# Weight sums and inverse softmax sums moved into the gate phase of a fused attention and GeGLU block

## The chip, the cores and the metric

The kernel runs on one core of one Trainium2 chip. The metric is the device time of one execution in microseconds (us), as the median of several runs. A separate, profiled execution gives the trace that is read here. Its engines are TensorE (PE; its weight loads are shown apart as PEld), VectorE (DVE), ScalarE (ACT), GpSimd (POOL) and SyncE (SP), whose queue issues all the transfers (DMA) that matter here.

## The reference

A block of 2048 tokens of width 640 is normalised, and two branches read the result: sliding-window attention of 32 heads of 20 (window 256), and a gated feed-forward part (GeGLU) of width 1728. Both are added to the input.

```python
qkv = (xn @ wqkv).reshape(B, S, 3, H, Dh)...
p = softmax(where(mask, q @ k.T * Dh ** -0.5, -1e9))
attn = (p @ v).reshape(B, S, D) @ wo
h = gelu(xn @ w_gate) * (xn @ w_up)
return x + attn + h @ w_down
```

All is float32. The kernel gets that precision from reduced-precision matmuls by splitting each operand into a high half (rounded) and a low half (the remainder), and adding three products: high by high, low by high, high by low.

## The kernel before

**Stages.** First the layer norm and the projections, with attention; parts of the gate and up projections are filled in between the attention's matmuls. Attention leaves, for each chunk c of 512 tokens, its unnormalised output in DRAM (`od[c]`, 640 rows) and the softmax sums (`sd[c]`, 32 heads). Then comes the *gate phase*, which computes the remaining feed-forward tiles f = 6 to 12 of 128 features and writes each to DRAM (`hd[f][c]`). Last, the *output phase* multiplies [h, attention output] with the stacked weights [w_down; wo] and adds x.

**Gate phase.** `gate_up_pair(f, w, p, extra)` handles tile f for the chunks 2p and 2p + 1, as a Winograd form of a 2 by 2 block product (fewer products, more sums): 54 matmuls of 128x128 by 512 (L858), into the banks pa, pb, pc, pe. Each tile has a first pair (p = 0) and a second (p = 1). VectorE adds up the results (`add`, L861): g1 from pb, `qp` from pc, then from pe, g2 from pc, u from pe. PE adds to the bank of pc a second time, so it must wait for the first `qp` sum. The products h2 and h1 (L891, L893) are stored by SP (L892, L894). `extra[i]` are functions put at four *hooks*, `more(0)` to `more(3)`, inside the pair, one for each quarter: there the next tile's weights are split (GpSimd makes their low halves) and summed, and in the last pair (f = 12, p = 1) the first work of the output phase is done.

**Output phase.** The stacked weights form nine *quads* q = 0 to 8. A quad is two blocks of 128 rows, each cut into two halves of 320 columns: four tiles of 128x320 (640 KB). There are eight groups p of 256 tokens, and a group has nine *steps*, one for each quad, and a small step "e" for the last 64 features (weights `w13`). Steps are counted n = 0, 1, ... through all groups. The quads 0 to 5 and the first block of quad 6 belong to h, the other five blocks to the attention output (`od`), which must be multiplied with the inverse softmax sums.

- Group 0 is *plain*: in a step four tiles of the quad as they are (kind "b"), 24 matmuls (L1023) into the banks 2, 3, 4, 8.
- The other groups are Winograd: 21 matmuls a step into seven banks, with three tiles of the quad and four *sums* of its tiles (kind "t"), and on the activation side with three parts and four sums `ss`. A group has 197 matmuls of 320 columns, step e among them; the plain group has 224.

`load_step(n)` loads a step's activations from `hd` and `od` (`hr`, 256 KB, L979). `split_step(n)` multiplies what comes from `od` with `rb` (the inverse sums, spread over the rows) on GpSimd (L1001), then makes high halves on ScalarE (L1003 in the plain group, L1007 and L1012 in Winograd ones) and sums and low halves on VectorE (the helper `sub`, L944). `fetch` loads a quad, `high_quad` (L929, L931) makes its high halves on ScalarE, `low_quad` (L941) its low halves on VectorE or GpSimd, and `sums_quad` turns the loaded tiles into the four sums in place (four subtractions of 128x320, VectorE, L944), which are split again as kind "t". All this is done in the steps 0 to 9: in the steps 1 to 5 a quad is split, summed and split again, in one step; in the steps 6 to 9 the quads 0 to 3, fetched a second time, are summed and split. `drain` adds a group's banks to x and stores it (L1053 and others; one of its sums is on GpSimd).

The inverse sums are made in the gate phase by `norm_items`: load `sd[c]`, reciprocal on VectorE, store to `rd[c]`. `load_rb` reads `rd[c]` back, spread, once for each chunk of the output phase (L984).

**What sets the order.** Within each phase, the order on PE, ScalarE, VectorE and the SP queue is that in which the program is written (`manual_schedule`), save that a few of the output phase's first splits stand inside the last gate pair. Every engine and the SP queue works in order: an instruction that waits holds all behind it. Transfers share eight semaphores in turn, so one waits until the eighth before it has landed.

**The loop of the output phase**, for each n: at the group's fourth step load x, then `load_step(n + 4)`, `split_step(n + 2)`, `prepare(n)` (the quad work of this step), and the matmuls, `terms`.

Of the kernel before, what the change touches and what calls it, by code (L numbers as in the profile page):

```python
# [60 lines left out]
def block_kernel(ctx, tc, x, wqk, wv, wgu, wdo, wdl, out):  # L61
# [22 lines left out]
    td = [{i: dram.tile([128, 2, C], F32, name=f"td{p}{i}") for i in (1, 2, 3, 4)} for p in range(NC // 2)]  # L84
    rd = [dram.tile([H, C], F32, name=f"rd{c}") for c in range(NC)]
# [671 lines left out]
    def norm_items(c):  # L757
        st = {}

        def n1():  # L760
            st["rc"] = c2.tile([128, 128], F32, name="rc", tag="rc", bufs=2)
            nc.sync.dma_start(st["rc"], sd[c].rearrange("h (a t) -> (h a) t", a=4))

        def n2():
            nc.vector.reciprocal(st["rc"], st["rc"])

        def n3():
            nc.sync.dma_start(rd[c].rearrange("h (a t) -> (h a) t", a=4), st["rc"])

        return n1, n2, n3  # L770

# [127 lines left out]
    borrow = {7: 0, 3: 4}  # L899

    def new_quad(kind, q):
        tag = place.get((kind, q))
        quads[kind, q] = (xp if tag else rp3).tile([128, 2, 4, HD], F32R, name=f"w{kind}{q}", tag=tag or f"w{kind}{q}")

    def slots(kind, q):
        if kind == "t" and q in borrow:
            return [(quads["b", borrow[q] + i], slice(1, 2), slice(i, i + 1)) for i in range(4)]
        if (kind, q) not in quads:
            new_quad(kind, q)
        return [(quads[kind, q], slice(0, 4), slice(0, 4))]  # L910

    def fetch(q, pool, tag, bufs):
        if pool is None:
            staged[q] = [wrp.tile([128, KT, 128], F32, name="wr", tag="wr") for _ in range(2)]
            staged[q] = [t.rearrange("p k m -> p (k m)").rearrange("p (h n) -> p h n", h=2) for t in staged[q]]
            for i, t in enumerate(staged[q]):
                nc.sync.dma_start(t, wdo[q][:, i].rearrange("p (h n) -> p h n", h=2))
        else:
            t = pool.tile([128, 4, HD], F32, name="stg", tag=tag, bufs=bufs)
            nc.sync.dma_start(t, wdo[q].rearrange("p k (h n) -> p (k h) n", h=2))  # L920
            staged[q] = [t]

    def high_quad(kind, q):
        n = 4 // len(staged[q])
        for i, raw in enumerate(staged[q]):
            for t, dst, src in slots(kind, q):
                if len(staged[q]) > 1:
                    dst = src = slice(n * i, n * i + n)
                    nc.scalar.activation(t[:, 0, dst], raw, AF.Copy)  # L929
                else:  # L930
                    nc.scalar.activation(t[:, 0, dst], raw[:, src], AF.Copy)  # L931

    def low_quad(kind, q, eng):
        n = 4 // len(staged[q])
        for i, raw in enumerate(staged[q]):
            for t, dst, src in slots(kind, q):
                if len(staged[q]) > 1:
                    dst = slice(n * i, n * i + n)
                else:
                    raw = staged[q][0][:, src]  # L940
                eng.tensor_tensor(out=t[:, 1, dst], in0=raw, in1=t[:, 0, dst].bitcast(F32), op=OP.subtract)  # L941
# [18 lines left out]
    for p in range(NP):  # L960
        ks_ = list(range(NQD))
        if p % 2:
            ks_ = ks_[4:] + ks_[:4]
        steps += [(p, k) for k in ks_[:4] + ["e"] + ks_[4:]]
    rbs = {}
# [15 lines left out]
    def load_rb(c):  # L981
        rbs[c] = cp.tile([128, C], F32, name="rb", tag="rb")
        for i in range(4):
            nc.sync.dma_start(rbs[c][32 * i:32 * i + 32], rd[c])  # L984

    def split_step(n):
# [11 lines left out]
        for i in range(2):  # L998
            if 2 * k + i >= NF - 1:
                a = raw[:, 2 * i:2 * i + 2].rearrange("p a t -> p (a t)")  # L1000
                nc.gpsimd.tensor_tensor(out=a, in0=a, in1=rbs[c][:, t0:t0 + 256], op=OP.mult)  # L1001
        if p == 0:
# [13 lines left out]
    def terms(n, ps, begin, end):  # L1016
# [3 lines left out]
        def mul(bank, parts):  # L1020
            last = len(parts) - 1
            for j, (a, b) in enumerate(parts):
                nc.tensor.matmul(ps[bank][:, 0:HD], a, b, start=begin and j == 0 and (k != "e"),  # L1023
                                 stop=end and j == last, skip_group_check=True)

        if k == "e":
            for bank, tok, h in ((2, 1, 0), (3, 1, 1), (4, 0, 0)):
                mul(bank, [(t[:, tok], w13[:, z, h * HD:h * HD + HD]) for z in range(2)])
            for z in range(2):
                nc.tensor.matmul(ps[8][:, 0:HD], t[:, 0], w13[:, z, HD:D], start=p > 0 and z == 0,  # L1030
                                 stop=p > 0 and z == 1, skip_group_check=True)
# [8 lines left out]
        if p == 0:  # L1040
# [3 lines left out]
        for bank, a, w, b in ((1, 0, wb, 0), (2, 2, wb, 2), (4, 1, None, 2), (5, 3, None, 0), (6, 4, None, 3),  # L1044
                              (7, 5, None, 1), (3, 6, wb, 3)):
            mul(bank, three(a, w, b))

    def drain(p, ps, xt):
# [18 lines left out]
        add(1, 1, a, nc.gpsimd)  # L1067
# [11 lines left out]
        add(2, 2, a)  # L1079
        store(2, 2)  # L1080
# [47 lines left out]
    for j, f in enumerate(range(NFA, NF - 1)):  # L1128
        end = f + 1 == NF - 1
        first, second = {i: [] for i in range(4)}, {i: [] for i in range(4)}  # L1130
        if j < NC:
            start_norm(j)
# [146 lines left out]
```

## Time and profile before

| what | value |
| --- | --- |
| median of 3 runs | 1148.94 us (1147.72 to 1149.1) |
| the profiled execution, own time | 1152.38 us |
| its span, first to last instruction | 1150.7 us |
| mean granted TensorE clock | 0.973 of full |
| PE busy | 1088.6 us (95%) |
| DVE busy | 757.4 us (66%) |
| ACT busy | 512.4 us (45%) |
| POOL busy | 403.7 us (35%) |
| moved by DMA | 136.75 MB, mean 119 GB/s |

How to read the views quoted below. The page cuts the span in 40 slices of 28.8 us and gives for each the busy share of every engine in tenths, and the granted TensorE clock in tenths. A view by windows has one line for each stretch: its length, then busy us (and number of instructions) of PE, PEld, DVE, ACT, POOL, then granted clock, DMA share and GB/s. A line of the waits reads: engine and tile that waited, whom it waited for, us in total, times, longest. A line of the timeline has start and length in us, engine, line, operation, output and inputs, shape, and in brackets the idle time before it and what ended it.

### The profile page before, as it was taken

Reading aid. Unit: us, or ns where it says so; the run is one execution under the profiler, and the core shown is the slowest. Engines: PE = TensorE matmul, PEld = TensorE weight load, DVE = VectorE, ACT = ScalarE, POOL = GpSimd, SP = SyncE. Lnnn points to the kernel's source line nnn. Section 1 sums busy time; section 2 is a strip of 40 time slices with the busy share of each in tenths; the row PEclk is TensorE's granted clock in tenths of the full one; section 3 lists DMA queues with packets and bytes.
Section 4 is the critical chain, followed back from the end, with each engine's and each line's share of the span. In section 5 each row is a group of like instructions: output and inputs, shape, how many; then the busy total and the mean of one; then the engine's idle time right before and its main releaser. Section 6 shows DMA issues by size and latency. Waiting matters only on the chain.

```text
span 1150.7 us, 20894 instructions
## 1 busy us (share of the span) xinstructions
PE 1088.6 (95%) x7241; PEld 871.0 (76%) x7241; DVE 757.4 (66%) x2064; ACT 512.4 (45%) x1034; POOL 403.7 (35%) x577
## 2 busy tenths in 40 slices
PE   8999999999999999999999999999975559999998
PEld 7877666666778666666666688888864449999998
DVE  7666666666666666666666366665545478888886
ACT  4435655656545556455555552232233233333332
POOL 5036634649445336553352411111112450202020
PEclk9999999999999999999999999999986779999999
DMA  5543343455532333533322152221064233444443
GB/s 195 185 130 100 110 135 108 120 148 161 153 96 71 113 114 111 165 100 112 112 84 89 61 183 81 79 91 62 37 213 140 97 106 116 133 141 132 143 125 103
DMA packets 87226, 136.75 MB, mean 119 GB/s; under 512 B 12608, under 2 KB 57280, under 8 KB 87120
## 3 DMA queue, kind: packets, MB, share of 16 engines
q1 hardware_dynamic: 87120, 135.41, 38.0%
q8 instruction: 57, 0.93, 0.4%
q14 instruction: 49, 0.40, 0.1%
HBM read 89.98 MB, written 45.09 MB: 117 GB/s over the span
## 4 chain that ended last, share of the span: by engine, by line
PE 82%; DVE 7%; issue 4%; DMA 3%; ACT 2%; POOL 1%; SPq 1%; DVEq 0%; POOLq 0%; ACTq 0%
PE ps_d L99 22%; PE ps L1023 18%; PE ps_g L858 14%; PE ps_o L514 7%; PE ps_e L492 7%; PE ps_m L440 6%; PE ps_v L99 5%; DVE junk L442 1%; PE ps_g L99 1%; DVE at L944 1%; DMA stg<-wdo 1%; DVE stg L944 1%; ACT P L494 1%; DMA xi<-x 1%; DVE xi L158 1%
## 5 line engine op out<-in xcount | busy, mean ns | idle before, releaser
L442 DVE CUSTOM_DVE_ANT_0 junk<-ps_m,mask 128x384 bf16<-128x384 f32 (+2 forms) x512 | 271.8, 531 | 177.3 <-PE ps_m L440 136.1
L494 ACT ACTIVATE P<-ps_e 128x512 f32<-128x512 f32 (+2 forms) x384 | 197.6, 568 | 63.6 <-PE ps_e L492 57.4
L1023 PE MATMUL ps<-wb,at 128*128 128x320 f32 x951 | 162.2, 324 | 36.3 <-ACT at L1003 19.2
L1023 PEld LDWEIGHTS ps<-wb,at 128*128 128x128 f32 x951 | 151.5, 199 | 40.4 <-ACT at L1003 20.8
L500 POOL TENSOR_SCALAR_AFFINE_SELECT P<-P 128x512 f32<-128x512 f32 x128 | 84.0, 656 | 176.1 <-ACT P L494 169.2
L99 PE MATMUL ps_d<-xh,wql 128*128 128x512 f32 x430 | 129.2, 410 | 0.0
L99 PE MATMUL ps_d<-xl,wqh 128*128 128x512 f32 x430 | 128.6, 408 | 0.0
L99 PE MATMUL ps_d<-xh,wqh 128*128 128x512 f32 x430 | 128.5, 409 | 0.0
L440 PE MATMUL ps_m<-ks,qs 120*128 120x128 bf16 (+1 forms) x704 | 121.0, 275 | 3.6 <-DVE mx L442 2.0
L492 PE MATMUL ps_e<-qs,ks 122*128 122x128 bf16 (+2 forms) x704 | 113.1, 277 | 1.5 <-ACT P L494 0.8
L1023 PE MATMUL ps<-wt,at 128*128 128x320 f32 x588 | 96.1, 313 | 0.0
L492 PEld LDWEIGHTS <-ks 122*128 122x128 bf16 x704 | 50.2, 98 | 55.1 <-issue 44.4
L1023 PEld LDWEIGHTS ps<-wt,at 128*128 128x128 f32 x588 | 89.6, 191 | 0.5 <-DVE m L944 0.2
L99 PEld LDWEIGHTS ps_d<-xh,wql 128*128 128x128 f32 x430 | 77.9, 189 | 15.7 <-issue 2.3
L99 PEld LDWEIGHTS ps_d<-xl,wqh 128*128 128x128 f32 x430 | 78.3, 189 | 14.9 <-issue 0.6
L99 PEld LDWEIGHTS ps_d<-xh,wqh 128*128 128x128 f32 x430 | 77.8, 189 | 14.1 <-ACT xh L183 0.3
L440 PEld LDWEIGHTS <-qs 120*128 120x128 bf16 x704 | 62.1, 98 | 32.8 <-issue 14.0
L503 POOL TENSOR_SCALAR_AFFINE_SELECT P<-P 128x512 f32<-128x512 f32 x112 | 72.6, 658 | 37.2 <-ACT P L494 37.2
L514 PE MATMUL ps_o<-P,v 128*32 128x384 f32 (+2 forms) x1408 | 84.3, 386 | 0.0
L223 POOL TENSOR_TENSOR pt<-r,pt 128x512 bf16<-128x512 f32 x40 | 46.8, 1170 | 80.9 <-ACT pt L222 80.8
L944 DVE TENSOR_TENSOR at<-hr,at 128x384 fp32r<-128x384 f32 (+1 forms) x72 | 51.0, 708 | 34.6 <-ACT at L1003 26.0
L1012 ACT ACTIVATE at<-ss 128x512 fp32r<-128x512 f32 x63 | 39.7, 630 | 72.3 <-DVE ss L944 72.1
(180 smaller groups left out, 1765.1 us busy)
## 6 DMA issues: line engine op xcount, KB each, us to landing
hd<-he SPq DMA_DIRECT2D x52, 256.0 KB
hr<-hd SPq DMA_DIRECT2D x104, 128.0 KB
wr<-wgu SPq DMA_DIRECT2D x27, 320.0 KB
qs<-qd SPq DMA_DIRECT2D x32, 240.0 KB
ks<-kd SPq DMA_DIRECT2D x32, 240.0 KB
stg<-wdo SPq DMA_DIRECT2D x11, 640.0 KB
xi<-x SPq DMA_DIRECT2D x16, 320.0 KB
qs<-qd SPq DMA_DIRECT2D x32, 160.0 KB
```

The source lines that it names most:

```text
L99: nc.tensor.matmul(ps, a(k), b(k), start=n == 0, stop=n == 3 * nk - 1)
L223: nc.gpsimd.tensor_tensor(out=pt[:, l, :], in0=r, in1=pt[:, 1, :], op=OP.subtract)
L440: nc.tensor.matmul(ps[:, lo:hi], lh, rhs, start=True, stop=True)
L442: nc.vector.tensor_tensor_reduce(out=junk[:, 0:n], in0=ps[:, 0:n], in1=mask[:, 384 - n:384], scale=1.0, scalar=NEG, op0=OP.add, op1=OP.max ...
L492: nc.tensor.matmul(ps[:, col:col + n], k[0:QROWS, j, kc:kc + 128], q[0:QROWS, j, q0:q0 + n], start=True, stop=True)
L494: nc.scalar.activation(pt[:, j, lo:hi], ps[:, lo:hi], AF.Exp, scale=SCALE)
L500: nc.gpsimd.affine_select(out=a, in_=a, pattern=[[0, 4], [1, 128]], compare_op=OP.is_ge, fill=0.0, base=0, channel_multiplier=-1)
L503: nc.gpsimd.affine_select(out=a, in_=a, pattern=[[0, 4], [-1, 128]], compare_op=OP.is_ge, fill=0.0, base=-1, channel_multiplier=1)
L514: nc.tensor.matmul(o[32 * j:32 * j + 32, q0:q0 + n], v[:, w0_:w0_ + 32], pt[:, j, col:col + n], start=i == 0, stop=i == len(todo) - 1, ski ...
L858: nc.tensor.matmul(ps, i, j, start=first and n == 0, stop=n == len(work) - 1, skip_group_check=True)
L944: nc.vector.tensor_tensor(out=o, in0=i, in1=j, op=op)
L1023: nc.tensor.matmul(ps[bank][:, 0:HD], a, b, start=begin and j == 0 and (k != "e"), stop=end and j == last, skip_group_check=True)
```

## The change

1. **Jobs in the gate phase.** A class `Job` has a load, items for VectorE and a store. Kind "r" is the reciprocal of a chunk's softmax sums (as before), kind "t" the four subtractions of a quad, which are now stored to DRAM (`wtd[q]`), and kind "o" multiplies three or two blocks of `od[c]` in place with the inverse sums and stores them back. `work(cap)`, put at the hooks, runs up to `cap` items of the first job, if its load was issued at least three hooks before, and starts the next job's load, with at most two jobs under way. There are 4 jobs "r", 9 "t" and 8 "o". `split_step` no longer multiplies, and `load_rb` is gone.
2. **Quad work in the output phase.** `tasks` gives each step at most one quad (of kind "b", or of kind "t" with the sums read from `wtd`): ScalarE's high half in step n, VectorE's low half in step n + 1, then the fetch three tasks ahead, into three buffers. GpSimd has no work left there.
3. **Group two** (p = 1) is plain for the quads 0 to 3 and Winograd for 4 to 8, so that the sums of the quads 0 to 3 are wanted only in group three. From group two on, the order of quads is 4 to 8, then 0 to 3 (before: only in every second group). Start and stop of the banks follow from lists (`begun`, `final`).
4. **The last gate pairs.** Quad 0 is fetched ahead of the last tile's first pair (before: ahead of its second), quads 1 and 2 around the second; the splits of steps 0 and 1 are both at the second pair's second hook, quad 1 is split at the third hook, quad 2 at the fourth.
5. `drain` makes its GpSimd sum on VectorE, and for group two adds bank 8.

```diff
+    wtd = [dram.tile([128, 4, HD], F32, name=f"wtd{q}") for q in range(NQD)]
...
-    borrow = {7: 0, 3: 4}
+    borrow = {7: 4, 3: 0}
...
-    def sums_quad(q):
-        t, = staged[q]
-        sub(t[:, 0], t[:, 1], t[:, 0])
-        sub(t[:, 1], t[:, 3], t[:, 1])
-        sub(t[:, 3], t[:, 3], t[:, 0])
-        sub(t[:, 2], t[:, 2], t[:, 3])
+    class Job:
+        def __init__(self, kind, i, ks=()):
+            self.kind, self.i, self.ks = kind, i, ks
+
+        def load(self):
+            kind, i = self.kind, self.i
...
+            elif kind == "t":
+                t = self.t = cp.tile([128, 4, HD], F32, name="ats", tag="at", bufs=3)
+                nc.sync.dma_start(t, four(wdo[i]))
+                self.items = [lambda: sub(t[:, 0], t[:, 1], t[:, 0]), lambda: sub(t[:, 1], t[:, 3], t[:, 1]),
+                              lambda: sub(t[:, 3], t[:, 3], t[:, 0]), lambda: sub(t[:, 2], t[:, 2], t[:, 3])]
+            else:
+                n = len(self.ks)
+                if self.ks[0] == 0:
+                    rbs[i] = c2.tile([128, C], F32, name="rb", tag="rb")
+                    for k in range(4):
+                        nc.sync.dma_start(rbs[i][32 * k:32 * k + 32], rd[i])
+                rows = self.rows = od[i][self.ks[0] * 128:(self.ks[-1] + 1) * 128].rearrange("(k p) t -> p k t", p=128)
+                t = self.t = cp.tile([128, n, C], F32, name="ato", tag="at", bufs=3)
+                nc.sync.dma_start(t, rows)
+                self.items = [lambda k=k: sub(t[:, k], t[:, k], rbs[i], OP.mult) for k in range(n)]
...
+    jobs = [Job("r", 0), Job("r", 1)]
+    for c, qs_, r in ((0, (4, 5), 2), (1, (6, 7), 3), (2, (8, 0), None), (3, (1, 2), None)):
+        jobs += [Job("t", q) for q in qs_] + [Job("o", c, (0, 1, 2)), Job("o", c, (3, 4))]
+        jobs += [Job("r", r)] if r else []
+    jobs.append(Job("t", 3))
...
+    def work(cap):
+        def fn():
+            hook[0] += 1
+            n = cap
+            while n and going and going[0][1] <= hook[0] - 3:
+                job = going[0][0]
+                job.items.pop(0)()
+                n -= 1
+                if not job.items:
+                    job.store()
+                    going.pop(0)
+            if len(going) < 2 and jobs:
+                job = jobs.pop(0)
+                job.load()
+                going.append((job, hook[0]))
+        return fn
...
+    def plain(p, k):
+        return p == 0 or p == 1 and k < 4
...
-        for i in range(2):
-            if 2 * k + i >= NF - 1:
-                a = raw[:, 2 * i:2 * i + 2].rearrange("p a t -> p (a t)")
-                nc.gpsimd.tensor_tensor(out=a, in0=a, in1=rbs[c][:, t0:t0 + 256], op=OP.mult)
-        if p == 0:
+        if plain(p, k):
...
-        add(1, 1, a, nc.gpsimd)
+        add(1, 1, a)
...
+        if j:
+            for i, n in enumerate((1, 3, 1, 1)):
+                first[i].append(work(n))
+        if not end:
+            for i, n in enumerate((2, 3, 1, 1) if j else (0, 0, 1, 1)):
+                second[i].append(work(n))
+        else:
+            fetch("b", 0, "wr")
         gate_up_pair(f, w, 0, first)
         if end:
+            while jobs or going:
+                work(1)()
             for n in range(2):
                 load_step(n)
-            fetch(0, cp, "stg", 1)
-            fetch(1, None, "", 0)
+            fetch("b", 1, "at")
...
-            second[0].append(lambda: quad(0, nc.vector))
-            second[1].append(lambda: [split_step(0), quad(1, nc.gpsimd), fetch(2, cp, "stg", 1), load_step(2)])
-            second[2].append(lambda: [split_step(1), quad(2, nc.vector), fetch(3, None, "", 0)])
+            second[0].append(lambda: quad(0))
+            second[1].append(lambda: [split_step(0), split_step(1), fetch("b", 2, "wr"), load_step(2)])
+            second[2].append(lambda: quad(1))
+            second[3].append(lambda: quad(2))
...
+    tasks = {0: ("b", 3), 1: ("b", 4), 2: ("b", 5), 3: ("b", 6), 4: ("b", 7), 5: ("b", 8), 6: ("t", 4), 7: ("t", 5),
+             8: ("t", 6), 9: ("t", 8), 10: ("t", 7), 12: ("t", 0), 13: ("t", 1), 14: ("t", 2), 20: ("t", 3)}
+    queue = list(tasks.values())
 
     def prepare(n):
-        if n == 0:
-            high_quad("b", 3)
-            low_quad("b", 3, nc.vector)
-            load_rb(0)
+        if n in tasks:
+            high_quad(*tasks[n])
+        if n - 1 in tasks:
+            low_quad(*tasks[n - 1])
+            if queue:
+                fetch(*queue.pop(0))
+        if n == 2:
             nc.scalar.activation(w13[:, 0], raw13, AF.Copy)
             sub(w13[:, 1], raw13, w13[:, 0].bitcast(F32))
-        if 1 <= n <= 5:
-            high_both(n + 3)
-            high_quad("t", n + 3)
-            low_quad("t", n + 3, nc.gpsimd)
-        if 6 <= n <= 9:
-            q = n - 6
-            sums_quad(q)
-            high_quad("t", q)
-            low_quad("t", q, nc.gpsimd)
...
+    fetch(*queue.pop(0))
+    load_step(3)
+    fetch(*queue.pop(0))
     raw13 = rp3.tile([128, D], F32, name="xr", tag="xr")
     nc.sync.dma_start(raw13, wdl)
-    for n in (4, 5, 6):
-        stage(n, n == 6)
-    load_step(3)
+    fetch(*queue.pop(0))
```

More of the change, by code (lines that the diff above doesn't have):

```diff
@@ L923, in high_quad, with four @@
[L923 to L941 removed]
+    def four(t):
+        return t.rearrange("p k (h n) -> p (k h) n", h=2)
```

131 lines of the change are left out of this document (68 added, 63 removed).

## Prediction

> **What bounds the kernel now.** I read the page's slices first, then windows of 20 us, then who waits for whom.
>
> ```profile
> PE   8999999999999999999999999999975559999998
> POOL 5036634649445336553352411111112450202020
> PEclk9999999999999999999999999999986779999999
> ```
> ```profile
> 820.00:840.00 20.00, 20.00 (x90) 16.57 (x89) 8.72 (x15) 4.34 (x10) 0.00 (x0) 1.00 0.26 92
> 840.00:945.00 105.00, 59.52 (x264) 53.33 (x263) 60.30 (x80) 33.47 (x45) 37.14 (x25) 0.72 0.39 132
> 945.00:1145.00 200.00, 200.00 (x1362) 199.53 (x1361) 166.79 (x444) 71.46 (x135) 31.28 (x39) 1.00 0.43 129
> ```
>
> TensorE (PE) is full before 840 us and after 945. In the 105 us between it works 59.5 us, and at a mean granted clock of 0.72. So the matmuls set the time, except in one hole: the last gate pair, the eight-bank opening of the output phase, and the change to its second group. The waits of 840 to 945 say who makes the hole:
>
> ```profile
> POOL wt L941 <- ACT wt L931: 56.5, 7, 25.1
> ...
> ACT wt L931 <- DVE stg L944: 28.7, 7, 5.4
> ...
> PE ps L1023 <- ACT at L1003: 19.2, 5, 4.8
> ACT at L1003 <- POOL hr L1001: 11.0, 3, 4.4
> ...
> PE ps L1023 <- DVE xr L1053: 10.2, 1, 10.2
> ...
> PE ps L1023 <- DVE at L944: 6.6, 4, 2.6
> ...
> PE ps_g L858 <- DVE qp L861: 6.0, 1, 6.0
> ```
>
> PE waits for activations (L1003), these for GpSimd's sums (L1001), GpSimd for ScalarE's weight halves (L931), ScalarE for VectorE's weight sums (L944). It is a ring of engines around two tasks per step (split a quad, sum it, split it again), not one slow engine. The SP queue's own waits add 39.0 us behind GpSimd (L920 <- POOL wt L941). And VectorE is slowed beside GpSimd:
>
> ```profile
> 926.73 2.92 POOL L941 TENSOR_TENSOR wt<-stg,wt 128x1280 fp32r<-128x1280 f32 x1 [4.75 <-ACT wt L931]
> ```
> ```profile
> 927.10 2.96 DVE L944 TENSOR_TENSOR at<-hr,at 128x384 fp32r<-128x384 f32 x1 [0.82 <-ACT at L1007]
> ...
> 1004.84 0.55 DVE L944 TENSOR_TENSOR at<-hr,at 128x384 fp32r<-128x384 f32 x1
> ```
>
> The same instruction takes 2.96 us while GpSimd runs its 2.92 us split, 0.55 us otherwise.
>
> **The floor.** PE's last undisturbed gate matmul ends at 840.88 us, its last matmul at 1145.31: 304.4 us. Without waits the changed kernel needs there: 18 gate matmuls at 0.2267 us (54 of a pair take 12.24 us) = 4.1; group one, 224 matmuls; group two, 4 plain steps of 24, 5 of 21 and 8 of the rest = 209 (197 before); six groups of 197. From the chain, 28.94 us lie between the L1030 pairs of 1013.85 and 1042.79, so a group is 28.94 and a matmul 0.1469: 224 + 209 give 63.6, six groups 173.6. Sum 241.3, so at most 63.1 us are to be had (12 extra matmuls, 1.8, are paid in it).
>
> **The change part by part.**
>
> *Sums and inverses moved into the gate phase.* It takes 36 subtractions (0.52 us apart, the four L944 stg of 871.29 take 2.07) and 40 GpSimd products (L1001, 0.80 each) out of the output phase, and puts 36 subtractions and 20 products 128x512 (0.60 apart, as L891 to L893) into VectorE's gate work: 31 us over some 135 us, in which VectorE is now about 60% busy. What hides them are idle moments of this shape:
>
> ```profile
> 823.99 0.69 DVE L861 TENSOR_TENSOR hr<-ps_g,gs 128x512 f32<-128x512 f32 x1 [1.02 <-PE ps_g L858]
> 824.59 0.41 DVE L820 TENSOR_TENSOR s3l<-sr,s3h 128x256 fp32r<-128x256 f32 x1
> 824.92 0.55 DVE L820 TENSOR_TENSOR s4l<-sr,s4h 128x384 fp32r<-128x384 f32 x1
> 827.38 0.69 DVE L861 TENSOR_TENSOR qp<-ps_g,q 128x512 f32<-128x512 f32 x1 [1.91 <-PE ps_g L858]
> ```
>
> The qp sum must end at 828.48, when PE adds to its bank again. So a first pair holds 1.91 + some 0.45 = 2.35 us of items before qp; followed through the job list, the fullest hooks put 2.4 there. A second pair, with no s3l, s4l, holds 3.2 and gets 2.8 at most. All fits if the data are there. Each item comes at least three hooks (9.2 us) after its load was issued. A landing takes from 4.1 us (stg issued 845.51, used 849.58) to 8.9 (hr issued 858.99, used 867.94, behind eight transfers). Added traffic is 23 MB over 140 us, 165 GB/s upon a mean of 72, where 348 to 377 have been moved. Bounds: 0, or 12 us if every one of the 17 loads (9 quads, 8 parts of the output) is 0.7 us later than the slack. I take 1.5, nearer the hidden end, since the load and slack rows leave it room. The 16 rb loads go along; in the output phase the first four held SP for 6.01 us (861.55). On SP every store waits for its items and hd stores and the next gate weights queue behind; those are used 12 us later, so it is free, and without that cover it is the same 0 to 12.
>
> *Last gate pair.* Before, quad 0 was fetched at 836.99 and held ScalarE to 842.68, VectorE's qp behind it, PE from 840.88 to 846.86. Now it is fetched a pair earlier. Next late are the activations of steps 0 and 1, also queued ahead of qp: issued 835.10 to 836.94; a later such load took 3.17 us to land (the chain's hr<-od at 923.40), and 512 KB of hd stores lie ahead, so 840.5; ScalarE 0.5, VectorE 0.6, 0.6 of them and qp 0.6: PE restarts at some 842.4, 1.6 us late (bounds 0 and 4).
>
> *Fetches at the start of the output.* Quad 2 is split after quad 1 (landing 842.7 as before, VectorE done 845.4), behind the second gelu: VectorE ends it near 849.0, then u, h2, h1 end near 850.8, against step 0 beginning at 842.4 + 4.1 = 846.5. On SP quad 3 stands behind the store of h1, at 851.2. Before, such a fetch landed 5.7 us later (856.87 to 862.55). Here 856.7: ScalarE 1.26 and 0.5 for the activations of step 3, VectorE 0.6 and 1.4: its low half is there at 860.6. PE wants it after three steps of 24 matmuls and two more, 10.9 us, at 857.3: 3.3 us late (bounds 0 and 7). Later quads have two steps to spare: three buffers, a fetch each 3.1 to 3.5 us of 640 KB with 256 KB of activations. At 370 GB/s and the steady 296 (172 GB/s at a share of 0.58) that is 1.7 + 0.9 = 2.6 us of transfer.
>
> *The clock.* The granted clock changes only at marks 3.41 us apart (846.06, 852.9, 866.54, 873.4 ...). A stretch with PE busy for 1.5 us of 3.4 (921.1 to 924.6) went to half; 1.7 (890.4 to 893.8) and 1.8 (917.7 to 921.1) kept it whole. So 1.6 us idle keeps the clock, 3.3 most likely loses it; after the wait at 864.6 PE ran at half from 868.6 to 873.4, 4.7 us, a loss of 2.4. I take that once (bounds 0 and 6).
>
> The Trainium skill ("TensorE: Matmul & The Clock Gate", "What's actually happening") has the clock halve after at least one idle window of about 3.4 us; by that, 3.3 us cost no clock and the sum would be 2.4 us better; the trace disagrees, since a window 45% busy was halved.
>
> *One split a step by ScalarE and VectorE alone.* In plain steps VectorE has 0.6 + 1.4 = 2.0 us against PE's 3.5, ScalarE 0.5 + 1.2. In group two's four Winograd steps VectorE has 2.3 (ss 1003.92 to 1006.23) + 1.4 = 3.7 against 3.1, and group one's four drain sums, 1.7, between. It starts two steps ahead and uses it up: some 1.5 us of waits near the group's change (bounds 0 and 4). The 10.2 us wait there (L1053) was VectorE behind stretched instructions; with GpSimd silent they are 0.55.
>
> *Drain on VectorE.* One more sum of 0.5 a group; VectorE is busy 167 of 200 us, so hidden in six groups; 0.4 in the tail.
>
> **Sum.** Gain 63.1 - 1.5 - 1.6 - 3.3 - 2.4 - 1.5 - 0.4 = 52.4 us. The profiled execution took 1152.38 us for its span of 1150.7, 3.4 above the median of the three runs shown; it gives 1152.4 - 52.4 = 1100.0, and the median 1148.94 - 52.4 = 1096.5.
>
> **Rivals.**
> 1. *The transfers become the bound* of steps 3 to 13. For it: eleven quads and the activations are 896 KB a step, and 660 to 680 us moved 208 GB/s at a share of 0.71. At 208 a step takes 4.3 us instead of 3.3, over 12 steps +12: 1108. Against: 348 to 377 GB/s when quads are in the queue.
> 2. *Half the hole stays*: the ring closes again, ScalarE waiting in order for a quad and the activations behind it. If each of steps 3 to 8 waits 2 us and loses the clock for it (6 x 2 + 10): 1118. Against: the split of step n+2 is queued ahead of quad work of step n.
> 3. *The gate phase jams; slower.* VectorE stands at an item whose load has not landed, qp behind it, PE behind qp, at a half clock after. Slower it gets when the 17 loads cost over 3.1 us each (52.4/17), that is 1.4 of wait and 1.7 of a halved stretch: landings over 9.2 + 0.9 + 1.4 = 11.5 us. The longest seen is 8.9. With 4 us each: 1096.5 + 68 = 1165. For it also: beside GpSimd the two he products (784.40, 785.86) take 1.5 instead of 0.68, and 56 more such operations can meet its splits. The Trainium skill ("SBUF — State Buffer", its ports) calls this an exclusive lock between GpSimd and VectorE operations with two SBUF inputs; nothing in the sum hangs on it.
> 4. *The change doesn't do it*: the jobs don't finish and are flushed in one go before the last pair. Followed hook by hook, the last (sums of quad 3) ends in the last hook of the last first pair; were it one job over, about 8 us: 1105. I count it to rival 1.
>
> **Chances.** Forecast 0.70 (its own range 1089 to 1104), rivals 1 and 4 together 0.15, rival 2 0.09, rival 3 0.06, of which a sixth near no change. The range, 1088 to 1113: the low end is nearly all of 63 us; the high end takes in rival 1 and the upper bounds of the gate and of quad 3. A difference of 0.2% is about what can be told from none here. Faster 0.94, same 0.01, slower 0.05.
>
> **What would show it.** PE's idle time of 840 to 945 falls from 45 to under 12 us, GpSimd is silent after the gate phase, and VectorE's at<-hr stays under 0.8 us. Step 3's wait is on a quad's low half; the wait before qp is on an hr load. Gate windows stay at 20.00 of 20 with VectorE near 15. The forecast is wrong if PE waits inside the gate windows, or waits for activations after step 4.

## The result, and the profile after

| | median, us | lowest to highest | runs |
| --- | --- | --- | --- |
| before, beside it | 1148.68 | 1147.72 to 1149.1 | 4 |
| changed | 1105.58 | 1104.18 to 1109.77 | 4 |

The ratio is 0.9632 (95% interval 0.9605 to 0.9659): faster by 43.1 us. The profiled execution of the changed kernel took 1106.18 us for a span of 1104.4, with a mean granted clock of 0.994 (before: 0.973).

The first view is the page's slices of the changed kernel, in tenths.

```profile
PE   8999999999999999999999999999999889999997
...
POOL 5045634567726435645525241111110000000000
PEclk9999999999999999999999999999999999999999
```

The hole in PE's row is filled but for two slices, no slice lost a tenth of its clock, and GpSimd has nothing to do in the output phase. The same three windows as before, with the same columns:

```profile
820.00:840.00 20.00, 20.00 (x90) 16.55 (x89) 14.14 (x25) 7.47 (x15) 0.00 (x0) 1.00 0.73 247
840.00:945.00 105.00, 97.44 (x618) 94.38 (x617) 75.81 (x150) 46.60 (x72) 0.00 (x0) 0.97 0.66 220
945.00:1100.00 155.00, 151.79 (x1027) 150.22 (x1025) 124.68 (x342) 53.34 (x101) 0.00 (x0) 1.00 0.38 119
```

From 840 to 945 us PE works 97.44 of 105 us instead of 59.52, at a clock of 0.97 instead of 0.72. In the gate window ahead of it VectorE went from 8.72 to 14.14 of 20 us and PE stays at 20.00. But from 945 on PE is no longer quite full (before: 200.00 of 200): of the 3.2 us that are missing, 1.5 lie behind the last matmul, and 1.7 are waits. Who makes PE wait, from 650 us to the end (the four largest):

```profile
PE ps L1064 <- DVE xr L1095: 3.2, 1, 3.2
PE ps L1064 <- ACT at L1035: 1.9, 1, 1.9
PE ps L1064 <- DVE m L930: 1.7, 5, 0.3
PE ps_g L844 <- DVE qp L847: 1.5, 2, 0.8
```

(L1064 are the output phase's matmuls, L1095 the sums of `drain`, L930 the helper `sub`, L1035 the activations' high halves of plain steps, L844 and L847 the gate matmuls and sums.) Nothing is left of the ring of 19.2, 10.2 and 6.6 us. The longest wait is 3.2 us. PE's timeline places the large ones:

```profile
847.02 10.72 PE L1064 MATMUL ps<-wb,at 128*128 128x320 f32 x72
859.61 0.41 PE L1064 MATMUL ps<-wb,at 128*128 128x320 f32 x1 [1.87 <-ACT at L1035]
...
861.74 5.03 PE L1064 MATMUL ps<-wb,at 128*128 128x320 f32 x22 [0.98 <-DVE wb L930]
...
889.87 0.89 PE L1064 MATMUL ps<-wb,at 128*128 128x320 f32 x3 [3.20 <-DVE xr L1095]
```

The output phase starts at 847.02, runs three steps (72 matmuls), and waits at step 3 for an activation and then for the low half of quad 3. The 22 matmuls behind that take 5.03 us instead of the 3.49 that the same 22 take in e1 below, at full clock: the clock was halved from 862.9 to 866.3. The next wait, 3.20 us, is the change to group two, where `drain` is late with freeing banks; the clock is halved behind it too, from 890.2 to 893.7.

**Where the time went.** The output phase takes 251.5 us to the end of the last matmul (847.0 to 1098.5), where 63.6 + 173.6 = 237.2 would do. Of the 14.3 us over that, 3.2 are at step 3, 0.4 at step e (its weights `w13`), 3.2 at the change of group, 3.4 lost in two stretches of 3.4 us at half clock, and 2.8 in the five groups from group four on, which take 29.50 us instead of 28.94 (5 x 0.56; group three takes 28.99); 1.3 is spread over what is left. The 29.50 is the distance of the same piece in the chain that ended last:

```profile
1012.57 21.94 PE ps L1064 x148
...
1039.62 0.88 DVE xr L1095 x2
1040.50 0.41 DVE m L930
...
1041.52 0.50 DVE m L930
1042.07 21.94 PE ps L1064 x148
```

At each change of group from group four on (five times: the pieces of PE begin at 953.57, 983.07, 1012.57, 1042.07 and 1071.57 us) the chain leaves PE, goes through VectorE's drain (xr and m) and comes back to PE. Before, this chain stayed on PE. That is the part of the loss in the steady groups, and the first question for the experiments. The second is the change to group two: what makes VectorE late there?

### The profile page after: what moved, and what is told of

Its sections match the earlier page's. It is cut to its first block, busy times and chain, and to the rows that moved or that the text cites. A ratio compares the mean times of both kernels' runs of the same rounds, so it can differ in the third digit from the quotient of the medians.

```text
span 1104.4 us, 20903 instructions
## 1 busy us (share of the span) xinstructions
PE 1077.3 (98%) x7253; PEld 861.5 (78%) x7253; DVE 758.3 (69%) x2088; ACT 510.0 (46%) x1030; POOL 335.2 (30%) x513
## 2 busy tenths in 40 slices
DMA packets 95913, 162.30 MB, mean 147 GB/s; under 512 B 13232, under 2 KB 57904, under 8 KB 95808
## 4 chain that ended last, share of the span: by engine, by line
PE 81%; DVE 8%; DMA 4%; issue 3%; ACT 2%; POOL 1%; SPq 1%; DVEq 0%; ACTq 0%
PE ps_d L100 22%; PE ps L1064 16%; PE ps_g L844 15%; PE ps_o L515 7%; PE ps_e L493 7%; PE ps_m L441 6%; PE ps_v L100 5%; DVE xr L1095 1%; DMA hr<-hd 1%; DVE junk L443 1%; PE ps_g L100 1%; ACT P L495 1%; DVE at L930 1%; PE ps_t L176 1%; DMA xi<-x 1%
## 5 line engine op out<-in xcount | busy, mean ns | idle before, releaser
L1064 PE MATMUL ps<-wb,at 128*128 128x320 f32 x999 | 158.2, 312 | 6.4 <-DVE xr L1095 3.2
L1064 PEld LDWEIGHTS ps<-wb,at 128*128 128x128 f32 x999 | 150.4, 190 | 7.4 <-DVE xr L1095 3.5
L1064 PE MATMUL ps<-wt,at 128*128 128x320 f32 x552 | 91.3, 313 | 1.7 <-DVE m L930 1.7
L1064 PEld LDWEIGHTS ps<-wt,at 128*128 128x128 f32 x552 | 84.1, 191 | 3.4 <-DVE m L930 3.0
L515 PEld LDWEIGHTS ps_o<-P,v 128*32 128x32 f32 x1408 | 40.1, 110 | 39.5 <-issue 29.2
L519 ACT ACTIVATE ob<-ps_o 128x512 f32<-128x512 f32 x32 | 19.1, 597 | 103.7 <-PE ps_o L515 50.8
```

The costliest lines, as they stand in the source:

```text
L515: nc.tensor.matmul(o[32 * j:32 * j + 32, q0:q0 + n], v[:, w0_:w0_ + 32], pt[:, j, col:col + n], start=i == 0, stop=i == len(todo) - 1, ski ...
L519: nc.scalar.activation(ob, o, AF.Copy)
L1064: nc.tensor.matmul(ps[bank][:, 0:HD], a, b, start=first, stop=last, skip_group_check=True)
```

## The experiments

All times are medians of at least four runs, with the ratio to the kernel before beside it. From one profiled execution to another the gate phase begins up to 2 us earlier or later, in the unchanged attention phase ahead of it (its first matmul at 671.1 to 675.1 us), so a difference of a microsecond or two between two kernels is read from the waits and the length of the output phase rather than from the totals. The changed kernel was not run again beside these; the kernel before was, with medians of 1148.8 to 1150.5 us.

| kernel | median, us | ratio [95%] | output phase, first to last matmul's start |
| --- | --- | --- | --- |
| changed | 1105.58 | 0.9632 [0.9605, 0.9659] | 251.2 |
| e1_gpsimd_sum | 1101.93 | 0.9585 [0.9560, 0.9610] | 247.9 |
| e2_sum_last | 1102.08 | 0.9583 [0.9552, 0.9613] | 245.9 |
| e3_order | 1105.76 | 0.9621 [0.9594, 0.9648] | 247.9 |
| e4_quad3_early | 1103.72 | 0.9593 [0.9561, 0.9625] | 249.1 |
| e5_no_quad_loads | 1096.19 | 0.9537 [0.9519, 0.9554] | 242.2 |
| e6_gpsimd_lows | 1110.58 | 0.9662 [0.9644, 0.9680] | 255.9 |
| e7_sums_late | 1117.05 | 0.9721 [0.9702, 0.9740] | 264.2 |
| e8_h_store_act | 1101.16 | 0.9580 [0.9564, 0.9596] | 247.5 |
| e9_x_later | 1101.98 | 0.9590 [0.9570, 0.9611] | 246.5 |
| e10_all | 1093.94 | 0.9527 [0.9514, 0.9541] | 241.9 |

### The steady groups: the drain's sum, or the order of quads?

The change moved one sum of `drain` from GpSimd to VectorE, and gave every group from the third on the order 4 to 8, 0 to 3. Either could have put VectorE on the chain. The first kernel gives the sum back to GpSimd.

```diff
-        add(1, 1, a)
+        add(1, 1, a, nc.gpsimd)
```

> Only the one sum of each drain (m into x, first half row) goes back to GpSimd. Theory (VectorE's drain is 0.5 us longer ahead of the sum that frees bank 7, and PE waits for that bank at each group's first step): the groups from three on take 28.94 us instead of 29.50, and PE's wait for DVE m is gone: 3 us less, about 1102.5. Rival (the new order of the quads, the same in every group, costs the 0.56 us): the groups stay at 29.5 and the time at 1105.6.

Measured: 1101.93 us, 3.7 below the changed kernel. The waits for `m` are gone, and the chain of e1 from 940 us to the last matmul is one piece of PE:

```profile
939.98 153.48 PE ps L1064 x1045
```

PE works 135.00 of the 135 us from 945 to 1080 (changed: 133.27). So it is this sum. Whether its amount (0.5 us a group) or its place costs, the second kernel tells: all sums stay on VectorE, but those that free banks 6 and 7 go into a tile of their own, ahead of the moved one.

```diff
+        m = rp3.tile([128, HD], F32, name="m2", tag="m2")
         nc.scalar.activation(a, b[1], AF.Copy)
         add(1, 1, b[2])
-        add(1, 1, a)
-        store(1, 1)
...
-        sub(a, b[6], a, OP.add)
-        add(1, 2, a)
-        sub(a, b[7], a, OP.add)
+        sub(m, b[6], a, OP.add)
+        add(1, 2, m)
+        sub(m, b[7], m, OP.add)
         add(1, 2, b[3])
         store(1, 2)
-        add(2, 1, a)
+        add(1, 1, a)
+        store(1, 1)
+        add(2, 1, m)
...
-        add(2, 2, a)
+        add(2, 2, m)
```

> The same sum stays on VectorE but is placed behind the sums that free the banks (a second small tile takes the running sum). Theory (place in the drain, not the amount of VectorE work): groups of 28.94 us, about 1102.5. Rival (VectorE's amount of work in a group is the limit): the groups stay near 29.5.

Measured: 1102.08, 3.5 below the changed kernel, the groups at 28.94 again and the chain one piece of PE from 939.93 to 1091.23 us. VectorE does as much as in the changed kernel (113.99 us of 135, against 111.92) and PE never waits for it. It was the place in the order, not the amount. (The intervals of e1 and e2 just overlap that of the changed kernel, so this reading rests on the traces.) The rival puts the old alternating order of quads back:

```diff
-        if p:
+        if p % 2:
```

> The quads' order alternates again from group three on (0 to 8 in every second group, as before the change); all else as in the changed kernel. Theory of the drain: the groups stay at 29.50 us and the time within 1 us of 1105.6. Rival (the order costs it): groups of 28.94, about 1102.5.

Measured: 1105.76, no difference from the changed kernel. Its waits for `m` stand as before (1.8 us in 5; at the change of group it waits 1.4, and 1.3 more at step e), and its groups are still 29.5 us apart (1010.65 and 1040.15 in its chain). The order falls as a cause of it.

This run also shows how much one profile says of the opening. Up to group one's drain, e1, e2 and e3 have the same program as the changed kernel. But their waits there differ. The wait at the change of group in e3:

```profile
889.28 0.71 PE L1064 MATMUL ps<-wb,at 128*128 128x320 f32 x3 [1.37 <-DVE xr L1095]
```

| one profiled execution each, us | changed | e1 | e2 | e3 |
| --- | --- | --- | --- | --- |
| step 3 | 3.2 | 2.7 | 2.2 | 1.3 |
| step e | 0.4 | 2.0 | 0 | 1.8 |
| change to group two | 3.2 | 2.9 | 2.7 | 1.4 |
| lost at half clock | 3.4 | 1.7 | 3.1 | 1.7 |
| sum | 10.2 | 9.3 | 8.0 | 6.2 |

So the sum varies by 4 us with no change in the program, and a difference of less than 2 us in one of these waits tells nothing. The five waits for `m` do not vary so: they are 0.3 to 0.4 us in every run that keeps the sum ahead of bank 7's.

### The change to group two: lateness handed on, transfers, or VectorE's load?

In the changed kernel VectorE has gaps ahead of its late drain. Its timeline:

```profile
859.59 0.69 DVE L930 TENSOR_TENSOR at<-hr,at 128x512 fp32r<-128x512 f32 x1 [7.29 <-ACT at L1035]
...
874.23 0.69 DVE L930 TENSOR_TENSOR at<-hr,at 128x512 fp32r<-128x512 f32 x1 [2.94 <-ACT at L1035]
...
889.33 1.67 DVE L1095 TENSOR_TENSOR xr<-ps,xr 128x320 f32<-128x320 f32 x4
```

It idles 13.2 us in three gaps up to 874 (the middle one, 2.92 us, ends at 864.60) and then works nearly without a break up to the drain at 889.33, which PE has been waiting for since 886.7. ScalarE, named as the releaser, was itself waiting for loads (1.89 us for hr<-od ahead of 873.57). Three causes could be told apart: that the late quad 3 hands its lateness on; that the loads of all the quads crowd the transfers; that VectorE simply has too much to do. The first kernel takes quad 3's lateness away: it is fetched in the last gate pair into tiles that have come free, and split at that pair's end; step 3's activations are loaded ahead of quad 4.

```diff
+        if where == "tp":
+            ts = [tp.tile([128, KT * 128], F32, name="own", tag=tag) for tag in ("xh02", "xl02")]
+            for i, t in enumerate(ts):
+                nc.sync.dma_start(t, wdo[q][:, i])
...
-            second[2].append(lambda: quad(1))
+            second[2].append(lambda: [quad(1), fetch("b", 3, "tp")])
...
+        if end:
+            quad(3)
```

> Quad 3 is fetched into freed tiles inside the last gate pair and split at its end, and the activations of step 3 are loaded ahead of quad 4. Both theories: step 3's waits of 3.2 us and the half clock after them go. Theory A (the 3.2 us wait at the change to group two is the first lateness handed on, by fetches that wait in the SP queue for VectorE): that wait and the half clock behind it go too, some 8 us in all, 1097. Theory B (it is VectorE's own load, 3.7 us a step against PE's 3.1 in the steps 8 to 11): a wait of 2 us or more stays there, 1101 or more.

Measured: 1103.72, by its interval not to be told from the changed kernel. Step 3's waits are gone and 1.7 us appear at step e; the wait at the change of group is still 3.0 us, and VectorE idles 7.80 and 3.42 us at the same places, up to 873.3. The lateness is not handed on by quad 3; the expectation of that theory missed. The next kernel leaves the loads of the later quads out altogether: every later split reads quad 3's tile, so its output is another.

```diff
+        if where == "stg" and (kind, q) != ("b", 3):
+            t = held[0]
...
+                staged[kind, q] = [(t, slice(0, 4))]
+            return
...
+        held[:] = [t]
```

> Leaves out the loads of all quads after quad 3 in the output phase (14 of 640 KB): every later split reads quad 3's tile, so VectorE, ScalarE and PE have the same instructions and the output is another. Theory A2 (the waits at step e and at the change to group two come from transfers that land late, so that VectorE idles some 12 us between 855 and 881 and then has too much left): both waits go, with the half clock behind them: 6 to 8 us less than the changed kernel, about 1098. Theory B (VectorE's load of the steps 8 to 11 alone): 2 to 3 us of wait stay at the change to group two, about 1102.

Measured: 1096.19, 9.4 below the changed kernel. PE's waits from 750 us on, but for one of 0.3 us:

```profile
PE ps L1072 <- DVE m L938: 1.7, 5, 0.3
PE ps_g L844 <- DVE qp L847: 1.0, 2, 0.8
PE ps L1072 <- DVE wb L938: 1.0, 1, 1.0
```

The wait for `xr` is gone, and so are ScalarE's 1.9 us at step 3, while VectorE does the same work in the same order. So VectorE's work by itself is hidden, and the loads are the cause of the wait at the change, be it that they land late or that the queue is held for their buffers (this run takes both away). What they meet in the changed kernel stands in its windows (last two columns: DMA share and GB/s):

```profile
870.00:875.00 5.00, 5.00 (x36) 5.00 (x35) 2.06 (x3) 1.91 (x2) 0.00 (x0) 1.00 0.99 356
```

They are full from 870 to 885 (356, 353 and 347 GB/s in three windows, at a share of 0.97 to 0.99) and were empty from 866.5 to 867.5 (0 GB/s), because the SP queue holds the next fetch until VectorE has freed a quad's buffer (its split of 865.05 ends at 866.54), and then issues a quad, the 640 KB of x (at 867.31) and the activations in one go:

```profile
866.61 0.33 SPq L908 DMA_DIRECT2D stg<-wdo  x1
...
868.26 0.57 SPq L1020 DMA_DIRECT2D hr<-od  x1
```

The last of these is used at 873.57, 5.3 us after its issue. (The 3.17 us of the prediction was such a load with little ahead of it.)

### What two parts of the change are worth

The first gives the low halves of the "t" quads back to GpSimd:

```diff
-            sub(t[:, 1, dst], raw, t[:, 0, dst].bitcast(F32))
+            (nc.gpsimd if kind == "t" else nc.vector).tensor_tensor(
+                out=t[:, 1, dst], in0=raw, in1=t[:, 0, dst].bitcast(F32), op=OP.subtract)
```

> Only the low halves of the nine quads of sums go back to GpSimd (2.9 us each there, 1.5 on VectorE). If taking GpSimd out was a main part of the gain: VectorE instructions beside it take up to 2.9 us again, and the time rises by 5 to 15 us, to 1110 to 1120. If the move of the sums was all: VectorE is relieved by 9 times 1.4 us, the wait at the change to group two shrinks, and the time is 1101 to 1106.

Measured: 1110.58, 5.0 above the changed kernel, with the wait at the change of group grown to 5.5 us (1.4 to 3.2 in the four executions above). Taking nine splits of 1.4 us off VectorE makes VectorE later:

```profile
880.18 3.04 POOL L927 TENSOR_TENSOR wt<-stg,wt 128x1280 fp32r<-128x1280 f32 x1 [0.87 <-ACT wt L923]
```
```profile
880.31 3.06 DVE L931 TENSOR_TENSOR ss<-hr 128x128 f32<-128x128 f32 x1
```

An operation that takes 0.28 us elsewhere lasts until GpSimd's split is over (it ends at 883.37, the split at 883.22), and so do others beside the other splits (3.21 and 2.97 us). The Trainium skill ("SBUF — State Buffer", "SBUF: two separate sides") calls this an exclusive lock held for a whole instruction; these rows agree with it. The second makes the four sums of each "t" quad in the output phase again, on VectorE alone, and leaves them out of the gate phase:

```diff
+    def sums_quad(q):
+        t, = whole[q]
+        sub(t[:, 0], t[:, 1], t[:, 0])
+        sub(t[:, 1], t[:, 3], t[:, 1])
+        sub(t[:, 3], t[:, 3], t[:, 0])
+        sub(t[:, 2], t[:, 2], t[:, 3])
...
+        if kind == "t":
+            sums_quad(q)
...
-        jobs += [Job("t", q) for q in qs_] + [Job("o", c, (0, 1, 2)), Job("o", c, (3, 4))]
+        jobs += [Job("o", c, (0, 1, 2)), Job("o", c, (3, 4))]
```

> The nine quads' sums are made in the output phase again, on VectorE, from the quad as it is (no jobs of kind t, same bytes loaded there); products with the inverse sums stay in the gate phase, GpSimd stays out. If moving the sums is a main part of the gain: 36 more subtractions of 0.52 us in the steps 6 to 20, of which PE sees those of the steps before the change to group two and in group two: 8 to 20 us more, 1114 to 1126. If not: within 3 us of 1105.6.

Measured: 1117.05, 11.5 above the changed kernel, with one wait of 9.84 us at the change of group and a clock of 0.90 from 840 to 945. Here VectorE is the bound: behind a gap of 4.08 us that ends at 870.8 it has none of a microsecond up to the drain at 893.42. So the sums' place in the gate phase is worth 11.5 us, and the gate phase gains little without them (its `qp` waits are 1.1 us instead of 1.5).

### A version without these waits

The quad that step 3 waits for is issued at 852.74, behind two stores of the last gate pair, and SP holds it until VectorE has made what they store:

```profile
852.33 0.32 SPq L880 DMA_DIRECT2D hd<-he  x1
852.74 0.41 SPq L908 DMA_DIRECT2D stg<-wdo  x1
```

The next kernel issues these two stores from ScalarE.

```diff
-        nc.sync.dma_start(hd[f][2 * p + 1], h2)
+        (nc.scalar if f == NF - 2 and p else nc.sync).dma_start(hd[f][2 * p + 1], h2)
...
-        nc.sync.dma_start(hd[f][2 * p], h1)
+        (nc.scalar if f == NF - 2 and p else nc.sync).dma_start(hd[f][2 * p], h1)
```

> Only the two stores of h in the last gate pair move from the SP queue to ScalarE's, so that quad 3 and all loads behind it no longer stand behind them (they were issued at 852.7, 5.7 us after PE began the output phase). Theory A2: quad 3 lands some 4 us earlier, step 3 waits under 0.5 us (3.2 before), step e's wait and that at the change to group two shrink to under 1.5 together: about 1098. Theory B: step 3's wait goes, but 2 to 3 us stay at the change to group two: about 1102.

Measured: 1101.16, 4.4 below the changed kernel. Step 3's waits and the halved stretch behind them are gone: 96 matmuls run in one piece where 72 did. The wait at the change of group, however, is 4.3 us, not under 1.5:

```profile
884.29 0.72 PE L1064 MATMUL ps<-wb,at 128*128 128x320 f32 x3 [4.25 <-DVE xr L1095]
```

PE ends group one 6.6 us earlier than in the changed kernel (880.0 instead of 886.7), and VectorE reaches its drain only 5.6 earlier (883.75 instead of 889.33): it still idles 3.52 us ahead of 868.18 for a load behind x and two quads. That suggested to load x of group one later, at its eighth step:

```diff
-        if i == 3:
+        if i == (3 if p else 7):
```

> The stores of h on ScalarE's queue (as in the run before) and, besides, group one's 640 KB of x loaded at the group's eighth step instead of its fourth, so that it no longer stands ahead of step 7's activations and of the quads in the SP queue. If late transfers set the wait at the change to group two (4.3 us there): step 7's activations land some 2 us earlier, VectorE idles 1.5 to 3 us less before 875, and the wait falls to 1 to 3 us: about 1099. If that load is hidden anyway: 4 us or more stay, 1101.

Measured, with the edit of e8 in it: 1101.98, not to be told from e8. The wait went from 4.3 to 3.1 us, less than it varies by itself, and in the profiled execution the gate phase began 3.4 us later than in that of e8. By itself this run settles nothing. The last kernel puts e8, e9 and e2 together, and two things more: the tasks of the quads 6, 7, 8, 0, 1 and 2 of kind "t" are up to two steps later (quad 7 at the same one), and the splits of the steps 0 and 1 come behind the last pair's `qp`.

```diff
-            second[1].append(lambda: [split_step(0), split_step(1), fetch("b", 2, "wr"), load_step(2)])
-            second[2].append(lambda: quad(1))
+            second[1].append(lambda: fetch("b", 2, "wr"))
+            second[2].append(lambda: [split_step(0), split_step(1), load_step(2), quad(1)])
...
-             8: ("t", 6), 9: ("t", 8), 10: ("t", 7), 12: ("t", 0), 13: ("t", 1), 14: ("t", 2), 20: ("t", 3)}
+             9: ("t", 6), 10: ("t", 7), 11: ("t", 8), 13: ("t", 0), 14: ("t", 1), 15: ("t", 2), 20: ("t", 3)}
```

> All together: stores of h on ScalarE's queue, x later, the drain's sum last on VectorE, the last pair's first splits behind qp, and the quads of sums 6, 7, 8 split one step later or two, so that 1.4 us less stand ahead of group one's drain. If the terms add: 3 (groups of 28.94 us) + 4.4 (step 3) + 2 to 4 (change of groups) + 0.7 (qp) less than the changed kernel: 1094 to 1096. If a wait only moves on: 1098 or more.

Measured: 1093.94 us (1093.48 to 1095.24 in five runs), ratio 0.9527 (0.9514 to 0.9541): 11.6 us below the changed kernel and 54.9 below the one before. PE's waits from 750 us on, but for one of 0.5 us at step e, and the two windows:

```profile
PE ps L1064 <- DVE xr L1095: 1.7, 1, 1.7
PE ps_g L844 <- DVE qp L847: 1.1, 1, 1.1
```
```profile
840.00:945.00 105.00, 102.72 (x674) 100.97 (x673) 83.64 (x171) 48.15 (x75) 0.00 (x0) 0.98 0.64 217
945.00:1080.00 135.00, 134.98 (x920) 134.68 (x919) 112.30 (x313) 50.10 (x94) 0.00 (x0) 1.00 0.43 134
```

If they add, the sums of e2 (3.5) and the stores of e8 (4.4) make 7.9 of the 11.6. The other 3.7 belong to the later x, the later tasks and the later splits together; they were not run one by one, and how they divide stays open. One profile doesn't show that the wait at the change became shorter by them: 1.7 us lies within the 1.4 to 3.2 of the same program.

## Why the prediction held, and where it was off

The forecast was 1096.5 us, and 1105.58 was measured: the mechanism held, the gain of 52.4 us came out as 43.1. The time lies in the stated range of 1088 to 1113, but 1.6 us above the 1104 that the forecast gave as its own upper end. Of the 9.1 us between, 6.2 are seen from profile to profile (1152.38 to 1106.18 is 46.2). The other 3 are not a step of the sum: the profiled execution of before lay 3.7 us above the median of its runs, that of the changed kernel 0.6, and which wait was longer in the former isn't shown. The 6.2 go by the terms of the sum as follows, in this one execution; the rows differ by 6.3 together.

| term of the sum | predicted, us | measured, us |
| --- | --- | --- |
| gate loads late | 1.5 | 1.3 |
| `qp` in the last pair | 1.6 | 0.9 |
| quad 3 late at step 3 | 3.3 | 3.2 |
| half clock | 2.4 | 3.4 (two stretches) |
| change to group two | 1.5 | 3.2 |
| sum of `drain` in six groups | 0 | 2.8 (five of them) |
| tail | 0.4 | 0.5 |
| step e (0.4), and scraps of the output phase | 0 | 1.7 |

**The floor and the hole: right.** PE lost 45 us of work time in 840 to 945 before and 7.6 now, the clock there rose from 0.72 to 0.97, and GpSimd is silent. VectorE's at<-hr, 2.96 us beside GpSimd, takes 0.55 to 0.69 everywhere. e6 and e7 show that both parts of this mattered: with GpSimd's splits back 5.0 us are lost, with the sums back in the output phase 11.5. That is 16.5 of the 43.1. How the rest divides over the products with the inverse sums, the plain steps of group two, the earlier fetches and the single split a step, no run shows.

**Gate loads: right in kind.** There is one wait in the gate phase proper, of 0.76 us at 755.3. From its first matmul to the point where PE adds to pc's bank again in the last first pair, the phase takes 156.34 us (673.30 to 829.64), before 155.05 (673.43 to 828.48). The timeline of VectorE shows the case that was feared, a product behind its load and `qp` behind the product:

```profile
754.71 0.69 DVE L930 TENSOR_TENSOR ato<-ato,rb 128x512 f32<-128x512 f32 x1 [1.11 <-DMA ato<-od]
755.32 0.68 DVE L847 TENSOR_TENSOR qp<-ps_g,q 128x512 f32<-128x512 f32 x1
```

It stopped PE like this once in 17 loads. Rival 3 needed 3.1 us for each of them, and falls.

**Last gate pair and step 3: right in the cause.** In the last pair PE restarted at 842.81 (forecast 842.4), 13.17 us behind the same point of the first pair, where 12.24 would do. Step 3's wait was forecast from the place of quad 3's fetch on SP behind the store of h1, with the fetch at 851.2, ScalarE's split at 856.7 and 3.3 us of wait. Measured were 852.74, 856.88 and 3.2; that the size fits so well is luck, since the same program waited 1.3 to 3.2 us there. The low half was there at 861.7 instead of 860.6, since the activation's load came 0.8 us after the split; PE was there 0.4 us later too, at 857.7. Two thirds of the wait show on the activation, which stands ahead of the low half on VectorE. The forecast had put it on the low half alone. e8 shows the cause: with the stores on another queue the wait is gone.

**Half clock: the size was off by its number.** It was taken once, for 2.4 us; it came twice, for 1.7 each, the second time behind the change of group (in e1 and e3 it came once, for 1.7). The wait of 1.5 us forecast there was thought to cost no clock, from the reading that 1.6 us idle keep it; a wait of 1.67 us in e10 did not. The Trainium skill ("TensorE: Matmul & The Clock Gate", "What's actually happening") halves the clock after at least one idle window of about 3.4 us. No wait of the changed kernel is that long (the longest is 3.20 us) and both stretches were halved, so the trace disagrees here as it did before.

**Change to group two: the step that counted only VectorE.** The prediction set VectorE's 3.7 us a step against PE's 3.1 and took 1.5. The measured 3.2 is one draw from 1.4 to 3.2, so the size alone would not refute it; the cause does. e5 shows that with the quads' loads away there is no wait at all, so the wait of 1.5 that it gave does not come from VectorE's work. What was missing is rival 1 in a milder form. The text took 2.6 us of transfer for each step's 896 KB as a mean and set them against 3.1 to 3.5 us of matmuls. But the queue doesn't run at its mean: it stands empty while the fetch waits for a buffer and is then full at some 350 GB/s, with the activations behind a quad and x. Loads that took 3.2 us by themselves took 5.3. The total lies nearer to rival 1's 1108 than to the forecast, and nearest to rival 4's 1105, by chance, since what rival 4 describes did not happen. But rival 1 spread its 12 us over the steps 3 to 13, and there is one wait, at the change; leaving the loads out gains 9.4 us, of which the forecast had most already, as quad 3's 3.3 and its clock's 2.4.

**Drain on VectorE: the mis-sized term.** "VectorE is busy 167 of 200 us, so hidden in six groups" was the step that failed. It cost 0.56 us in each of five groups, 2.8 in all, in every profile that has it so. It is the one loss that clearly stands out of the spread: the forecast's 3.3, 2.4 and 1.5 for step 3, half clock and change make 7.2, and the same places, with step e, for which the sum had no term, took 6.2 to 10.2. e1 and e2 show why: the sum stands ahead of the two that free banks 6 and 7, and PE waits for bank 7 when it has done 15 matmuls of the next group. An engine with a sixth of its time idle can still be on the chain for the few microseconds in which another waits for its order of work.

**Rivals 2 and 4** did not come about: no wait for activations after step 3 reached PE, and no jobs were flushed ahead of the last pair: the last subtraction of a job is at 832.50, inside the last first pair, and PE works 20.00 of 20 us from 820 to 840.

**Its own tests.** GpSimd silent, at<-hr below 0.8 us, the wait of `qp` on an hr load, idle time below 12 us from 840 to 945: these came true. The wait of step 3 on a low half came true for 1.0 of its 3.2 us; the rest was on the activation. Of the signs of being wrong, "PE waits inside the gate windows" came true once, for 0.76 us.

## What to carry to other kernels

A share of busy time doesn't tell whether one more operation on an engine is free: look at the few microseconds where another engine waits for it (here the banks at the change of group), and put the new operation behind what releases others. When transfers are costed, don't set a mean rate against a mean step: see where an in-order queue holds a fetch for a buffer, because what it issues afterwards lands in one heap. Work that doesn't depend on the stage that is short of an engine can go into a stage where that engine idles, even at the price of a trip to DRAM: here 25.6 MB more were moved (162.30 instead of 136.75), and the kernel became 43 us faster. And before a wait is explained by an edit, see how much it varies with the same program.

## What the runs showed of the hardware

- A wait of 1.67 us was followed by half the granted clock: in e10 PE is idle from 878.6 to 880.3, and the windows behind it show 0.50 from 881.4 for 3.4 us.
- In e1, 2.65 us of waits in three pieces, between 858.1 and 861.6, cost no clock at all (1.00 in each half microsecond from 855 to 868). In e2 the same three waits were shorter, 2.25 us between 857.9 and 861.0, and the clock was half from 860.4 to 867.2. Whether a stall costs clock thus hangs on how it falls as well as on its length; where the marks lie in each of these runs was not worked out.
